# A planned four-batch attention-and-FFT-convolution kernel: complex products of the last batch summed on TensorE, a row scale moved into tables, split output tiles, and a new order of the work

## The chip, the cores and the metric

One core of a Trainium2 chip. The metric is the time of one execution of the program in device microseconds (us); lower is better. Times of a kernel are given as the median of its runs.

## The reference, cut to what matters

Four batches; 8 heads, 768 positions, head size 64. Attention is banded: each row sees the 8 first keys and the 96 keys up to itself, with a slope bias per head. Its output, 768 x 512 per batch, goes into a gated long convolution: a projection to three parts, a circular convolution of the second part with a filter along the sequence by a real FFT, a product of all three, and an output projection.

```python
scores = scale * np.matmul(q, k.transpose(0, 1, 3, 2)) + bias      # kept: global or local keys
a = softmax(scores); x = np.matmul(a, v)                           # -> (B, 768, 512)
proj = x @ w_proj; x1, x2, x3 = the three parts of proj
x2_conv = np.fft.irfft(np.fft.rfft(x2, axis=1) * np.fft.rfft(filter_fft, axis=0), axis=1)
out = (x1 * x2_conv * x3) @ w_out
```

## The kernel before, in words

The whole kernel is a graph of operations (class `Plan`) that is written out once and then issued in an order that stands in the source as a string, `ORDER` (L41). Each word names an operation by number and the engine that takes it: P is PE, A is ACT, V is DVE, G is POOL, S is SP. The digits behind a P are the PSUM banks that it takes. Every engine works through its own words strictly in this order; where an operand is not there, it waits and everything behind it on that engine waits too. A word such as `i5b2` is a filler (`busy`, L305): five matmuls of 512 columns on a buffer of zeros (`idle`, a part of the tile `uw`), whose result nobody reads. The order before has 12 such matmuls in four words, all in the first 16 us.

The stages of one batch, by names and lines:

- Loads (`load`, L324). Batch 0's first two pairs of heads of q and k come over SP's queue as float32 into a staging tile and are cast by DVE or ACT (`FIRST`, L206). All other loads go over POOL's queue, which casts to 16 bits as it moves; POOL's loads use eight semaphores in turn, so a load waits until the one eight places before it has landed. v of batch 0 comes in seven tiles, behind the pairs and the filter.
- Transposes of q and k on PE (`turned`, L677 and L680; the second form, 12 half-height matmuls a pair, is for pairs that POOL loaded), copied out to `QT` and `KT`. For the last batch SP's DMA transposes take their place.
- Scores on PE (L729), for batch 0 with the bias added by two further matmuls (`near`, L723), exponential on ACT (L744), mask product on DVE (L761; not for batch 0), in three groups of key tiles.
- Values (L779, L784) on PE, with a row sum; division on DVE or ACT (L803, L807), transposes back (L824) into `xT`.
- Gates (L902): four matmuls of 384 columns each, 64 groups in all; ACT scales one part out (`x1`), DVE multiplies it with the other, straight out of PSUM (L916, `g`).
- Butterflies on DVE (L831 on), the projection of the convolution branch (L965), copied out by L969 with a row scale `part` on four of six copies (tile `ab`), forward transform (L1081) against the tables `fold` and `fwd`, copied to `X` (L1084).
- Products with the filter's spectrum on DVE: p1 = X h1, p2 = X h2 (L1099, L1102), and the sums of the complex product X = p1 - p2, p1 + p2 (L1107, L1108).
- Inverse transform on PE (L989, L992): four matmuls of 128 columns a group, against the tables `inv` and `inr`; those come from PE transposes of the forward tables (`inverse_tables`, L523) and seven scaled copies. Then mixing on DVE, product with the gate (L1070), output projection (L1021): four matmuls of 512 columns a tile, six tiles a batch, copy (`ot`) and store over SP.

Setting up takes constant fills by memsets on DVE (`gaps`, `ones`, `second`, `part`) and sine tables on ACT.

Of the kernel before, what the change touches and what calls it, by code (L numbers as in the profile page):

```python
# [17 lines left out]
P = 128  # L18
NG = 8
# [9 lines left out]
def act(n):  # L29
    return 0.06 + n / 1200.0  # L30
# [11 lines left out]
0V 1V 2A 3G 4V 5V 30V 34V 45S 8V i3b5 17P0 18A 19V 57S 22P1 47S 12P2 49S 9V 32G 51S 55G 23A 58A 11V 13A 53G 7G  # L42
46V 20V 54G 33V 35G 50V 43V 24V 37V 21A i1b5 84P0 38A 48A 14V 60S 82P3 88P4 56G 85A 73G 61G 83A 52V 36V i3b5
96P3 116P67 15V 25V 98P01 89A 39V 97A 90P4 41V i5b2 94P5 16A 62G 26A 86P3 59V 44V 99A 10V 42V 91V 40A 117A 95V
92P2 63G 27V 122P45 156P01 31V 123A 93V 87V 104P67 65G 210V 120P45 29V 157A 102P23 105A 121A 67G 100P67 154P45
64G 103A 111P23 101A 66G 211V 245G 28V 212V 213V 155A 112V 244G 214V 113V 215V 118P01 152P67 119A 106P45 107V
150P01 129P23 216V 236G 246G 79A 153A 235G 151A 75A 243G 163P67 68G 130V 124P01 232G 108V 131V 109P4 77A 237G
158P23 114P5 110A 80A 164V 125V 165V 132P4 69G 166P6 126V 6V 217P7 115A 127P0 223P5 133A 219P4 159V 167V 346P6
238G 81A 160V 78A 220A 224A 348P1 128V 161P2 233G 138P0 218A 193V 194V 228P45 241G 134P7 140A 338P0 349V 231G
162A 136A 221P1 196V 347V 230A 240G 185V 381P67 222A 234G 359P23 340P5 339V 139P0 360A 135P1 195V 184V 419P23  # L50
187V 70G 382A 229A 141V 341V 361V 334P6 420A 172P0 76A 168P7 137V 174A 239G 472G 170A 353P23 421V 335V 375P45
242G 197V 471G 169P1 383V 74A 336P0 198V 146P6 186V 72G 376A 247G 462G 173P7 344P4 337V 354A 461G 342P0 249S
175V 250G 410P23 148A 345A 350P67 411A 142P5 188V 343V 199V 171V 189V 144V 351A 202P4 356P01 71G 412V 416P23
357A 254G 372P67 251G 253G 270P5 190V 252G 200V 373A 225P01 417A 201V 226A 191V 192V 257P6 227A 377V 258V 271A
463G 206V 470G 259P2 413P01 378P67 464G 260A 255G 272P5 207V 352V 283P2 465G 563P3 208A 374V 358V 414A 285P0
355V 204V 248S 379A 143P1 286A 284A 469G 564A 466G 273A 367P67 476G 415V 147P0 205A 209A 274P2 458G 380V 145V
203A 368V 263P3 149V 264A 362P01 276P5 261P4 275A 287V 277A 369V 363V 467G 418V 364V 468G 389P67 262A 278P2
573P3 384P45 265P0 390V 279A 370P2 288V 574A 180P1 266A 371A 391V 473G 475S 565P3 427P67 566A 280V 385V 281V
386V 282V 571P0 460G 567P2 256G 459G 697G 479G 422P45 182A 568A 268V 365P1 572A 423V 366A 428V 424V 176P3 267V
569P2 178A 570A 181P0 644P45 429V 177P1 291P2 645A 695G 183V 292A 430P6 387P7 179V 638P45 269V 431A 392P2 691G  # L60
425P3 388V 603P01 639A 301P6 297P7 393V 299P2 604A 457G 426V 300A 303P3 581P45 302A 582A 561P0 298A 704G 646V
293P2 640V 701G 688G 480G 449V 294A 687G 406P1 696G 394P6 703G 693G 584P45 448V 304A 289P7 396A 407P3 408V
295P6 451V 450V 698S 562A 705G 296A 398P2 585A 395P0 559P6 605V 477G 452V 409V 682G 586V 453V 400A 600P45
578P23 403P1 290A 560A 397V 305V 306V 481G 597P67 454V 601A 690G 598A 482P0 402P4 307V 579A 432P5 575P23 404A
483A 683G 474S 583V 405V 606P67 694G 308V 434A 495P4 576A 635P01 607A 641P23 399P5 456V 455V 444P6 636A 592P01
497P7 496A 577V 642A 446A 580V 498A 686G 508P4 637V 478G 700G 433P2 401V 593V 692G 309V 602V 587P67 699S 509A
510P3 702G 594A 435V 486P4 608V 588V 436P2 501P5 511A 438A 684S 310V 643V 311V 599V 589A 445P0 484P1 312V
499P2 485A 512V 500A 652P67 447V 689G 487A 653V 503P2 502A 488P3 609P01 313V 490P4 489A 504A 437P5 610V 685S
440P3 491A 654V 611A 505V 506V 614P67 615V 513V 439V 786S 616A 788S 319P2 442A 507V 647P01 441P5 612P4 785S
314V 648V 492V 613A 590P6 595P7 493V 649V 322P3 617P4 320A 655P2 596A 494V 315V 528P7 618A 591A 316P4 524P6  # L70
443V 784S 650P0 783S 529A 631P7 656A 323A 651A 790S 674V 317A 522P3 792S 520P2 673V 789S 523A 676V 787S 526P0
516P1 623P4 633A 517A 521A 625A 518P3 527A 624P7 514P2 675V 793S 796P45 632P1 515A 619P2 525A 626V 677V 797A
805P67 519A 621A 806A 634V 678V 719P4 802P23 799P01 530V 679V 531V 794S 620P5 622V 720A 669P4 734P6 627P5 681V
800A 827P01 803A 671A 735A 804V 821P23 828A 798V 680V 807V 629A 628P4 818P67 630V 822A 801V 824P01 532V 819A
708P5 813P23 820V 791S 795S 825A 814V 533V 706P4 815V 709A 707A 856P01 657P5 534V 712P4 857A 862P23 829V 823V
865P01 659A 859P67 670P5 863A 826V 535V 858V 860A 866A 710P2 672V 665P3 830P67 808P01 711A 861V 713A 714P2
864V 667A 831V 715A 723P4 809V 721P5 536V 832A 810V 732P2 724A 816P3 537V 817A 666P0 835P67 867V 717V 727P4
668V 722A 331P3 324S 728A 725P4 318S 658P5 811P0 538V 836V 733A 716V 660V 332A 873P23 726A 661P1 730V 837A
718V 874V 868P45 328P6 869V 321S 736V 325P7 663A 812A 662P0 729V 870V 838P1 875A 871P4 539V 833P5 333S 731V
876P2 839A 541P3 737V 834A 852P5 740P1 872A 877A 844P2 742P4 854A 752P5 326A 746P7 664V 741A 895V 894V 748P0  # L80
540V 896V 743A 753A 747A 749A 897V 898V 738P1 899V 547P4 750P7 744P5 745A 556P0 848P5 739A 751A 903P7 916P1
755V 900V 846A 327S 754V 901V 902V 845P2 904A 850A 917A 853P5 931P1 329A 756V 542A 929P6 932A 847V 920P7 757V
918P1 921A 930A 919A 907P7 924P6 330S 922P1 908A 550P2 905P7 543S 855V 923A 758V 911P1 933V 759V 925A 553P6
548A 906A 912A 934V 909P7 760V 927V 926V 557A 882P3 841P0 763V 928V 544P1 910A 884A 840P3 914V 956P7 941P4
545A 842A 551A 952P1 887P5 913V 761V 552S 915V 953A 554A 849P2 957A 762V 935P1 942A 851V 954P6 950P3 955A
939P7 951A 936A 764V 555S 959V 940A 546S 843V 765P4 937P3 777P2 774P0 886P1 958V 768P7 938A 549S 888A 944V
771P1 772A 943V 878P3 960V 945V 780P6 961V 946V 769A 558S 962V 947V 766A 963V 948V 778A 891P7 964V 889V 949V
880A 967V 965V 767S 968V 966V 883P1 775A 890P3 773S 781A 978V 770S 879P0 975P6 892A 980V 776S 893V 972P7 881V
885V 981V 969P1 976A 979V 782S 779S 973A 977S 982P0 983V 974S 970A 971S 984S 985P1 988P7 986A 991P6 987S 989V
992A 990S 993S  # L90
# [108 lines left out]
class Fused:  # L199
    PERIOD = 40.0  # L200
    NEAR = 3
    TWICE = frozenset()
# [3 lines left out]
    FIRST = (("k",0),("q",0),("k",1),("q",1))  # L206
# [29 lines left out]
    def buffers(self):  # L236
# [25 lines left out]
        self.inv = t("inv", [P, 4, P])  # L262
        self.uw = t("uw", [P, 4, 2, 2, P])
# [49 lines left out]
    def times(self, e, out, in_, c):  # L313
        if e == "A":
            self.nc.scalar.mul(out, in_, c)  # L315
        else:
            self.nc.vector.tensor_scalar(out, in_, c, None, op0=Alu.mult)

# [99 lines left out]
    def setup(self):  # L418
# [25 lines left out]
        def part(_):  # L444
            for i in range(2):
                c = math.sqrt(0.75) * (1.0 - 2.0 * i)
                v.memset(self.part[0:64, 2 * i:2 * i + 1], 1.0)
                v.memset(self.part[64:P, 2 * i:2 * i + 1], c)
                v.memset(self.part[0:64, 2 * i + 1:2 * i + 2], c)
                v.memset(self.part[64:P, 2 * i + 1:2 * i + 2], 1.0)  # L450
        g.op("V", 0.5, part, w=["part"], bias=-100)
# [4 lines left out]
        for i in range(4):  # L456
            et = self.E[i]

            def gaps(_, et=et):
# [4 lines left out]
            g.op("V", 0.42, gaps, w=[("E", i, c) for c in range(3)], name="gaps", bias=-3300)  # L464

    def tables(self):
# [3 lines left out]
        for a, n in enumerate((512, 256, 512)):  # L470
# [7 lines left out]
            g.op("V", dve(n, 2), lambda _, th=th: nc.vector.tensor_scalar(  # L478
                th, th, MAGIC, -float(S), op0=Alu.subtract, op1=Alu.mult), r=[("th", a)],
                w=[("th", a)], bias=-9898)  # L480
            g.op("V", dve(n), lambda _, th=th, b=b, n=n: nc.vector.tensor_add(
# [41 lines left out]
    def inverse_tables(self):  # L523
# [16 lines left out]
        for i, (dst, rows, lo, hi, k) in enumerate((  # L540
# [6 lines left out]
                 lambda e, dst=dst, rows=rows, lo=lo, hi=hi, k=k: self.times(  # L547
                     e, dst, corners(b.f16()) if lo is None else b.f16()[rows, lo:hi], k), use=[b],
                 w=[("inv", i)])

    def distances(self):


# [694 lines left out]
```

## Time and profile before

| what | value |
|---|---|
| median of 3 runs | 169.41 us (168.69 to 169.66) |
| the profiled execution's own time | 169.03 us |
| its span, first to last instruction | 167.3 us |
| outside the span | 1.73 us |
| mean granted TensorE clock | 0.996 |
| matmuls on PE, of these fillers | 1591, 12 |
| POOL's DMA issues | 84 |

A row of the chain of waits or of the timeline gives start, length, engine and line, and a count behind an x. The timeline's lengths are each instruction's own, and neighbours overlap in the pipeline; the chain's lengths are laid end to end, so it shows what one instruction adds to a dense stream. A row of the groups gives the count, the summed busy time, the mean of one in ns, and the idle time ahead of them.

### The profile page before, as it was taken

What the parts mean: (1) busy time and instruction counts of PE and PEld (TensorE: products, weight loads), DVE (VectorE), ACT (ScalarE), POOL (GpSimd) and SP (SyncE); (2) the same over time, 40 slices, a digit from 0 to 9 for tenths busy, and PEclk for the clock granted to TensorE, in tenths of its full rate; (3) what the DMA queues carried; (4) which work ended last, traced back from release to release, by engine and by line L of the source; (5) the groups of instructions that cost most, each with busy time, mean ns of one, the idle gap of its engine ahead of it and who ended that gap; (6) DMA issues with size and microseconds to landing.
All of it is one profiled execution on the core that took longest, in us unless ns stands there. A gap on an engine that the chain in (4) does not pass through costs nothing.

```text
span 167.3 us, 4244 instructions
## 1 busy us (share of the span) xinstructions
PE 158.4 (95%) x1591; PEld 93.5 (56%) x1591; DVE 154.2 (92%) x364; ACT 149.6 (89%) x324; POOL 76.3 (46%) x100
## 2 busy tenths in 40 slices
PE   7679999999999999999999999999999999999990
PEld 2335349666645777645556674455577644565550
DVE  4597999999999999999999999999989999999951
ACT  4949999999999999999999999999999879792851
POOL 7996699999769995989930000000000000000000
PEclk9999999999999999999999999999999999999998
DMA  4999999999999999999999645300010111052595
GB/s 157 246 183 200 153 151 165 162 171 174 166 159 125 120 119 155 155 155 144 149 143 153 77 95 136 149 0 0 4 65 4 65 60 66 4 217 97 205 358 191
DMA packets 84957, 22.14 MB, mean 132 GB/s; under 512 B 75585, under 2 KB 81993, under 8 KB 84937
## 3 DMA queue, kind: packets, MB, share of 16 engines
q0 software_dynamic: 72768, 11.92, 95.0%
q1 hardware_dynamic: 12168, 9.97, 20.0%
q8 instruction: 12, 0.20, 0.5%
q14 instruction: 9, 0.07, 0.1%
HBM read 25.40 MB, written 6.29 MB: 189 GB/s over the span
## 4 chain that ended last, share of the span: by engine, by line
PE 37%; POOL 20%; DMA 19%; ACT 12%; DVE 5%; issue 3%; POOLq 0%; ACTq 0%
DMA vn<-in_v_dram 13%; PE bank L902 11%; PE bank L1021 11%; POOL kn L327 7%; POOL qn L327 6%; DMA qn<-in_q_dram 5%; PE bank L965 5%; ACT xn L807 4%; POOL vn L327 3%; ACT E L744 3%; PE bank L989 2%; ACT ab L315 2%; ACT X L311 2%; POOL w L327 2%; PE bank L1081 2%
## 5 line engine op out<-in xcount | busy, mean ns | idle before, releaser
L902 PE MATMUL bank<-xT,w 128*128 128x384 f16 x256 | 49.5, 326 | 0.2 <-ACT ab L315 0.2
L744 ACT ACTIVATE E<-bank 128x864 f16<-128x864 f32 x48 | 42.1, 955 | 0.5 <-PE bank L729 0.3
L902 PEld LDWEIGHTS <-w 128*128 128x128 f16 x256 | 23.4, 98 | 16.3 <-issue 1.5
L327 POOL DMA_DIRECT2D vn<-in_v_dram x28 | 26.7, 965 | 3.5 <-DMA wo<-in_moe_w_out_dram 1.8
L1021 PE MATMUL bank<-wo,y 128*128 128x512 f16 (+1 forms) x100 | 23.4, 370 | 0.1
L327 POOL DMA_DIRECT2D kn<-in_k_dram x25 | 22.0, 900 | 3.0 <-PE bank L729 2.4
L327 POOL DMA_DIRECT2D qn<-in_q_dram x24 | 20.9, 883 | 1.3 <-DMA vn<-in_v_dram 1.2
L761 DVE TENSOR_TENSOR E<-E,mask 128x864 f16<-128x864 f16 x36 | 20.7, 601 | 0.0
L315 ACT ACTIVATE x<-bank 128x384 f16<-128x384 f32 x30 | 17.0, 572 | 2.0 <-PE bank L902 1.8
L315 ACT ACTIVATE ot<-bank 128x512 f32<-128x512 f32 (+1 forms) x23 | 13.4, 611 | 5.3 <-PE bank L1021 5.3
L916 DVE TENSOR_TENSOR g<-bank,x 128x384 f16<-128x384 f32 x32 | 17.4, 552 | 0.3 <-PE bank L902 0.2
L965 PE MATMUL bank<-w,xs 128*128 128x512 f16 x64 | 15.9, 379 | 0.1
L779 PE MATMUL bank<-vn,E 128*128 128x65 f16 x224 | 15.6, 193 | 0.3 <-ACT xn L807 0.2
L729 PE MATMUL bank<-QT,KT 64*128 64x216 f16 (+2 forms) x224 | 15.3, 243 | 0.1
L784 PE MATMUL bank<-vn,E 128*128 128x65 f16 x192 | 15.3, 193 | 0.0
L779 PEld LDWEIGHTS <-E 128*128 128x128 f16 x224 | 14.2, 97 | 2.0 <-issue 0.2
L311 ACT CAST eo<-bank 128x384 f16<-128x384 f32 x32 | 14.4, 551 | 0.5 <-PE bank L992 0.4
L311 ACT CAST X<-bank 128x512 f16<-128x512 f32 x24 | 14.5, 658 | 0.0
L1021 PEld LDWEIGHTS <-y 128*128 128x128 f16 x100 | 9.3, 98 | 8.8 <-issue 0.4
L784 PEld LDWEIGHTS <-E 128*128 128x128 f16 x192 | 13.3, 97 | 1.4 <-issue 0.7
L729 PEld LDWEIGHTS <-KT 64*128 64x128 f16 x224 | 7.8, 94 | 10.7 <-issue 8.2
L807 ACT ACTIVATE xn<-bank,rc 128x64 f16<-128x64 f32 x60 | 13.6, 480 | 0.0
(160 smaller groups left out, 334.1 us busy)
## 6 DMA issues: line engine op xcount, KB each, us to landing
out_dram<-ot SPq DMA_DIRECT2D x23, 256.0 KB
vn<-in_v_dram POOLq DMA_DIRECT2D x28, 120.0 KB, 7.3
kn<-in_k_dram POOLq DMA_DIRECT2D x16, 96.0 KB, 4.9
qn<-in_q_dram POOLq DMA_DIRECT2D x16, 96.0 KB, 4.9
w<-in_moe_w_proj_dram POOLq DMA_DIRECT2D x4, 256.0 KB, 5.3
kn<-in_k_dram POOLq DMA_DIRECT2D x7, 120.0 KB, 6.4
g<-in_moe_filter_fft_dram POOLq DMA_DIRECT2D x1, 768.0 KB, 9.3
qn<-in_q_dram POOLq DMA_DIRECT2D x6, 128.0 KB, 5.3
```

Source lines behind the costliest of these rows:

```text
L311: {"A": nc.scalar.copy, "V": nc.vector.tensor_copy, "G": nc.gpsimd.tensor_copy}[e](out, in_)
L315: self.nc.scalar.mul(out, in_, c)
L327: return self.g.op(eng, 0.57 + 0.00035 * nbytes[0] if eng == "G" else 0.5, lambda _: e.dma_start(dst, src), w=w, r=r, nbytes=nbytes, name= ...
L729: nc.tensor.matmul(bs[hh].f32()[:, off:off + w], self.KT[hs, hp, P * m:P * m + P], self.QT[hs, hp, KL * m:KL * m + w], start=(off == 0 and ...
L744: g.op("A", act(864), lambda _: nc.scalar.activation(eo, bs[0].two()[:, :, 0:432].rearrange("p h (m w) -> p h m w", m=2), Act.Exp, scale=s ...
L761: g.op("V", dve(864, 2), lambda _: nc.vector.tensor_mul(eo, eo, mk), r=[("mask", 2 * hp), ("mask", 2 * hp + 1)], w=[("E", hp, gi)], name=" ...
L779: nc.tensor.matmul(o[:, n, hh], ef[:, at:at + P], vt[:, t, 2 * hp + hh, 0:D + 1], start=first, stop=(t == 0), skip_group_check=True)
L784: nc.tensor.matmul(o[:, n, hh], ef[:, at:at + P], vt[:, t - 1, 2 * hp + hh, 0:D + 1], start=False, stop=True, skip_group_check=True)
L807: nc.scalar.mul(to[:, i, n], o[:, i, n, 0:D], rc[:, i, n])
L902: nc.tensor.matmul(bk.f32()[:, 0:h], self.w[:, c, o + P * j:o + P * j + P], self.xT[:, c, h * s:h * s + h], start=(c == 0), stop=(c == 3))
L965: nc.tensor.matmul(bk.f32(), src[:, c], w[:, c, DM:2 * DM], start=(c == 0), stop=(c == 3))
L1021: nc.tensor.matmul(bk.f32()[:, 0:n], y[:, c, P * t:P * t + P], self.wo[:, c, cs], start=(c == 0), stop=(c == 3))
```

## The change

Seven edits and a new order string:

1. `SUMPE = (3,)`: for batch 3 the sums of the complex product (L1107, L1108) are left out. Each inverse group takes p1 and p2 themselves: one matmul with p1 against `inv`, one with p2 against `inv` or a negated copy of it, `neg`, accumulated in PSUM. So 6 matmuls a group instead of 4, in 8 groups.
2. The row scale `part` leaves the copies `ab` and goes into the table `fold` (an operation `foldp`, four scalings of 128 x 128). It has to wait until the inverse tables were taken from the unscaled `fold`; the forward transforms wait for it.
3. `SPLIT = (3,4,5)`: the last batch's last three output tiles are issued as two PE operations of two matmuls a bank each, one for each half of y's channels.
4. `TWICE` for batch 3: ACT copies the second gate part out of PSUM, and DVE multiplies two 16-bit tiles in SBUF.
5. `FIRST` loses q of pair 1: it comes over POOL's queue in place of SP's, needs no cast, and takes the 12 half-height transposes.
6. Constant fills may run on ACT (`fill`), as may one step of the sine tables.
7. `ORDER` is new: on POOL the loads stand in another sequence; the inverse tables' transposes stand in the first PE operations; and the fillers are now 55 matmuls, in words of 1 and 2 at the start, and of 30, 8 and 14 later. PE has 1656 matmuls.

```diff
-0V 1V 2A 3G 4V 5V 30V 34V 45S 8V i3b5 17P0 18A 19V 57S 22P1 47S 12P2 49S 9V 32G 51S 55G 23A 58A 11V 13A 53G 7G
...
+0V 1V 2A 3G 45S 30A 47S 4V 34V 6A 9A 32G 56S 49S 5V i1b5 22P0 55G 23A 54G 7G 24A 10V 17P1 8V 33V 25V 51G 18A
+35G 19A 12P2 13A 46V 52G 37A 48V i2b5 83P0 38A 53G 81P3 72G 20V 26A 61G 63G 21A 14V 44V 50V 15V 39V 201P1 93P2
...
+353V i30b6 349P0 145P6 75A 174V 249S 412A 348V 141P2 346V 254G 357P45 350V 228A 417P01 147A 375V 253G 420P67
...
+359V 260P2 386V 365V 387V 462G 560P3 287A 479G 478G 285A 469G 261A i8b7 368P45 381V 279P0 366P1 472G 561A 473G
...
+i14b3 428P45 266P1 390P67 257G 265A 706G 567A 562P0 281V 267A 429V 388P3 391V 563A 179P2 430V 564P1 392V 176P4
...
-    TWICE = frozenset()
+    SPLIT = (3,4,5)
+    SUMPE = (3,)
+    TWICE = tuple((3,j,s) for j in range(4) for s in range(2))
...
-    FIRST = (("k",0),("q",0),("k",1),("q",1))
+    FIRST = (("k",0),("q",0),("k",1))
...
+    def fill(self, to, value):
+        n = to.shape[0]
+        zero = self.idle[0:n, 0:math.prod(to.shape[1:])]
...
+        self.nc.scalar.activation(to, zero, Act.Copy, bias=value, scale=1.0)
...
+        def scaled(e):
+            for s in range(4):
+                f = self.fold[:, (s + 2) % 4]
+                self.times(e, f, f, self.part[:, s:s + 1])
+        g.op("AV", {"A": 4 * act(P), "V": 4 * dve(P, 4)}, scaled, r=["part"], w=[("fwd", 3), "foldp"], name="foldp")
...
-                g.op("AV", self.evac(512), lambda e, i=i, t=t, k=k, bk=bk: self.times(
-                    e, self.ab[i][:, t, :], bk.f32(), k), use=[bk], r=["part"], w=[("ab", i, t)],
+                g.op("AV", self.evac(512), lambda e, i=i, t=t, bk=bk: self.copy(
+                    e, self.ab[i][:, t, :], bk.f32()), use=[bk], w=[("ab", i, t)],
...
-                            nc.tensor.matmul(to, X[:, s, cs],
+                            apart = b in self.SUMPE and not z
+                            k, c = s // 2, s % 2
+                            nc.tensor.matmul(to, self.p1[k][:, c, cs] if apart else X[:, s, cs],
                                              self.inr[:, s - 4] if z else self.inv[:, (s + 2) % 4],
                                              start=(n == 0), stop=True, skip_group_check=True)
+                            if apart:
+                                nc.tensor.matmul(to, self.p2[k][:, 1 - c, cs],
+                                                 self.inv[:, (s + 2) % 4] if c else self.neg[:, k],
+                                                 start=False, stop=True, skip_group_check=True)
...
+                parts = ((0, 1), (2, 3)) if last and t in self.SPLIT else (range(4),)
...
-                r=[("ab", i, t), ("fwd", 1 if s > 3 else 3)])
+                r=[("ab", i, t), ("fwd", 1) if s > 3 else "foldp"])
...
+        if b in self.SUMPE:
+            return
```

More of the change, by code (lines that the diff above doesn't have):

```diff
@@ L47 @@
[L47 to L51, printed above, removed]
@@ L442, in setup, with part @@
             None, op0=Alu.add), r=["irow"], w=["rows"], bias=-9988)
-        def part(_):
+        def part(e):
             for i in range(2):
                 c = math.sqrt(0.75) * (1.0 - 2.0 * i)
[L447 to L451, printed above, removed]
+                for rows, cols in ((slice(0, 64), (1.0, c)), (slice(64, P), (c, 1.0))):
+                    for x in range(2):
+                        to = self.part[rows, 2 * i + x:2 * i + x + 1]
+                        if e == "A":
+                            nc.scalar.activation(to, self.idle[rows, 0:1], Act.Copy, bias=cols[x], scale=1.0)
+                        else:
+                            v.memset(to, cols[x])
+        g.op("AV", {"A": 0.5, "V": 0.5}, part, r=["idle"], w=["part"], name="part", bias=-100)
         def ident(_):
@@ L457, in setup, with gaps @@
             et = self.E[i]
-            def gaps(_, et=et):
+            def gaps(e, et=et):
+                if e == "A":
+                    self.fill(et[:, :, 0:1488].rearrange("p h (m w) -> p h m w", m=6)[:, :, :, 216:248], 0.0)
+                    self.fill(et[:, :, 1456:1536], 1.0)
+                    return
                 et = et.bitcast(F32)
@@ L463, in gaps @@
                 v.memset(et[:, :, 728:768], ONES)
-            g.op("V", 0.42, gaps, w=[("E", i, c) for c in range(3)], name="gaps", bias=-3300)
+            g.op("AV", {"A": act(384) + act(160), "V": 0.38}, gaps, r=["idle"], w=[("E", i, c) for c in range(3)], name="gaps", bias=-3300)
     def tables(self):
@@ L477, in tables @@
                 w=[("th", a)], bias=-9899)
[L478 to L481, printed above, removed]
-                th, th, b.f32()[:, 0:n]), use=[b], r=[("th", a)], w=[("th", a)], bias=-9897)
+            g.op("AV", {"A": act(n), "V": dve(n, 2)}, lambda e, th=th: nc.vector.tensor_scalar(
+                th, th, MAGIC, None, op0=Alu.subtract) if e == "V" else nc.scalar.activation(
+                th, th, Act.Copy, bias=-MAGIC, scale=1.0), r=[("th", a)], w=[("th", a)], bias=-9898)
+            g.op("V", dve(n), lambda _, th=th, b=b, n=n: nc.vector.scalar_tensor_tensor(
+                th, th, -float(S), b.f32()[:, 0:n], op0=Alu.mult, op1=Alu.add), use=[b], r=[("th", a)],
+                w=[("th", a)], bias=-9897)
             o = (self.fold if a == 2 else self.fwd[:, 4 * a:4 * a + n // P]).rearrange("p s r -> p (s r)")
@@ L549, in inverse_tables @@
                  w=[("inv", i)])
+        def scaled(e):
[3 more added lines that the diff above has]
+        g.op("AV", {"A": 4 * act(P), "V": 4 * dve(P, 4)}, scaled, r=["part"], w=[("fwd", 3), "foldp"], name="foldp")
+        g.op("AV", {"A": 2 * act(P), "V": dve(2 * P, 4)}, lambda e: [self.times(
+            e, self.neg[:, n], self.inv[:, 2 - 2 * n], -1.0) for n in range(2)] if e == "A" else self.times(
+            e, self.neg[:, ::-1], self.inv[:, 0:4:2], -1.0), r=[("inv", i) for i in range(7)], w=["neg"], name="neg")
     def distances(self):
@@ L569, in distances, with second @@
         self.ahead = [g.op("G", 2.0, first, w=["dg"], bias=-9970)]
-        def second(_):
-            v.tensor_copy(dg[:, n:2 * n], dg[:, 0:n])
-            v.tensor_copy(dg[:, 2 * n:2 * n + 168], dg[:, 0:168])
-            v.memset(dg[0:NG, n:600], -HUGE)
-            v.memset(dg[0:NG, n:n + KL], -float(NL))
-            v.memset(dg[0:NG, 2 * n:2 * n + KL], -float(NL))
-            v.memset(dg[0:NG, 600:648], -float(NL))
-        g.op("V", dve(216, 4) + dve(168, 4) + 1.0, second, r=["dg"], w=["dg2"], bias=-3500)
+        def second(e):
+            put = self.fill if e == "A" else v.memset
+            self.copy(e, dg[:, n:2 * n], dg[:, 0:n])
+            self.copy(e, dg[:, 2 * n:2 * n + 168], dg[:, 0:168])
+            put(dg[0:NG, n:600], -HUGE)
+            put(dg[0:NG, n:n + KL], -float(NL))
+            put(dg[0:NG, 2 * n:2 * n + KL], -float(NL))
+            put(dg[0:NG, 600:648], -float(NL))
+        g.op("AV", {"A": 1.24, "V": 1.24}, second, r=["dg", "idle"], w=["dg2"], name="second", bias=-3500)
         g.op("V", 0.12, lambda _: v.memset(far, 0.0), w=["far"], bias=-3600)
@@ L956, in conv @@
         for i in range(2):
-            for t, (src, key, k) in enumerate((
-                    (self.xo[:, i], ("xo",), 1.0),
-                    (self.xs[:, 3 * i], ("xe", "xd"), self.part[:, 2 * i:2 * i + 1]),
-                    (self.xs[:, 2 - i], ("xe", "xd"), self.part[:, 2 * i + 1:2 * i + 2]))):
+            for t, (src, key) in enumerate((
+                    (self.xo[:, i], ("xo",)), (self.xs[:, 3 * i], ("xe", "xd")), (self.xs[:, 2 - i], ("xe", "xd")))):
                 bk = g.bank()
@@ L981, in conv @@
                     cs = slice(P * (2 * jp + jj), P * (2 * jp + jj) + P)
+                    apart = b in self.SUMPE
+                    src = [("p1", par), ("p2", par), ("X", 4 + par), "neg"] if apart else [
+                        ("X", s) for s in slots]
                     def turn(_, bk=bk, cs=cs, slots=slots, par=par):
@@ L1123, in load_first, with ones @@
         vt = self.vn[0]
-        def ones(_, vt):
+        def ones(e, vt):
+            if e == "A":
+                self.fill(vt[:, 0, :, self.D:], 1.0)
+                self.fill(vt[:, 1:, :, self.D:self.D + 2], 1.0)
+                return
             self.nc.vector.memset(vt[:, 0, :, self.D:].bitcast(F32), ONES)
@@ L1128, in load_first @@
         for i in range(2):
-            self.g.op("V", 0.4, lambda _, i=i: ones(_, self.vn[i]), w=[("vn1", i)], name="ones", bias=-4400 + 1400 * i)
+            self.g.op("AV", {"A": act(256) + act(96), "V": 0.33}, lambda e, i=i: ones(e, self.vn[i]), r=["idle"], w=[("vn1", i)], name="ones", bias=-4400 + 1400 * i)
         self.distances()
@@ L1180, in graph @@
         self.spectrum()
-        self.early = [x for x in g.ops if x.name in ("near", "angles", "mask")]
+        self.early = [x for x in g.ops if x.name in ("near", "angles", "mask", "gaps", "ones", "second", "part")]
         for b in range(self.B):
```

109 lines of the change are left out of this document (60 added, 49 removed).

## Prediction

> **What bounds the kernel now.** I read the page first: busy shares, the slices, the shares of the chain of waits.
>
> ```profile
> PE   7679999999999999999999999999999999999990
> ...
> DVE  4597999999999999999999999999989999999951
> ACT  4949999999999999999999999999999879792851
> ...
> PEclk9999999999999999999999999999999999999998
> ...
> PE 37%; POOL 20%; DMA 19%; ACT 12%; DVE 5%; issue 3%; POOLq 0%; ACTq 0%
> ```
>
> Three engines look full from slice 4 on, so shares decide nothing, and a busy PE is not PE at its peak. So the chain in order of time comes next. It runs through POOL's loads until 71.7 us, then from engine to engine, and from 110.8 us to the last matmul at 163.54 through PE alone. It also gives the price of one matmul in a dense stream.
>
> ```profile
> 72.32 0.48 PE bank L729 x8
> ...
> 111.81 0.80 PE bank L729 x18
> ...
> 115.39 0.06 PE bank L779 x2
> ...
> 126.13 1.14 PE bank L824 x20
> ...
> 150.02 1.73 PE bank L1021 x8
> ...
> 155.64 2.60 PE bank L902 x16
> 158.24 5.23 PE bank L1021 x28
> 163.54 0.38 ACT ot L315
> ```
>
> A matmul of 512 columns costs 1.73/8 = 0.216 us, of 384 columns 2.60/16 = 0.1625, of 128 columns 1.14/20 = 0.057, one for the values (65 columns) 0.06/2 = 0.03, a half-height score 0.80/18 = 0.044 to 0.48/8 = 0.060. The timeline of PE in the first 26 us shows the fillers and the start of the values:
>
> ```profile
> 9.82 1.49 PE L307 MATMUL bank<-uw 128*128 128x512 f16 x3
> ...
> 14.15 1.25 PE L307 MATMUL bank<-uw 128*128 128x512 f16 x5
> ...
> 25.27 0.20 PE L779 MATMUL bank<-vn,E 128*128 128x65 f16 x1
> ```
>
> At 25.27 the values of batch 0's third tile group begin.
>
> **The ruler.** I count PE's matmuls from that group on, in each program's own order, at these prices. Before: 256 of 384 columns (41.6 us), 224 of 512 (48.4), 8 of 256 (0.9, half price), 346 of 128 (19.7), 376 values (11.3), 168 half-height scores at 0.052, the middle (8.7; 7.4 to 10.1): 130.6 us. The trace takes 163.54 - 25.27 = 138.3. So PE loses about 7.7 us (6.3 to 9.0) to waits in that stretch, and since the chain is PE alone after 110.8, nearly all of it lies before that.
>
> **The change, part by part.**
>
> *Fillers and order.* 52 of the 55 new filler matmuls stand behind that group of values: 30 after 14 us of further work, then 8 and 14. They cost 52 x 0.216 = 11.2 us of PE, whatever else PE might be waiting for. They are free where PE would have waited; beyond that each pushes the end. 11.2 is more than the 7.7 that were lost before.
>
> Is there a wait of 6.5 us at the block of 30? The instruction behind it transposes k of pair 3 of batch 1. Its second load is POOL's 31st in the new order. The 31st before, issued at 32.97, took 4.8 us to land:
>
> ```profile
> 17.80 0.85 POOL L327 DMA_DIRECT2D kn<-in_k_dram  x1 [2.44 <-PE bank L729]
> ...
> 32.97 2.56 POOL L327 DMA_DIRECT2D kn<-in_k_dram  x3
> ...
> DMA to landing us min/median/max: 4.8/4.8/4.8
> ```
>
> That is 37.8 us. PE's work from the values group to the block is 14.1 us: 28 gate matmuls 4.55, 10 of 512 columns 2.16, 70 of 128 columns 4.0, 64 values 1.9, 28 scores 1.5. From 23.5 (below) PE reaches the block at 37.6, when the load is landing. So the block covers almost nothing of that load and holds back k's copy on DVE, the scores behind it, and everything that DVE has queued behind that copy. Later waits on DVE and ACT shrink by as much, since those two run ahead: that is how 11.2 us of fillers can swallow most of the 7.7.
>
> *The start.* Values of the third group need all seven tiles of v. The view of that tile in the first 30 us:
>
> ```profile
> L327 POOL DMA_DIRECT2D vn<-in_v_dram x7: 901/903/1197, 8.8 to 14.5; - x7
> ...
> DMA to landing us min/median/max: 8.8/9.1/9.9
> ```
>
> The last is issued at 14.5 and lands at 23.3. The new order puts the same pairs, filter and v tiles ahead of it; q of pair 1 only changes its queue. So 23.3 stays, and PE, which otherwise reaches the group earlier now (inverse tables and near scores stand ahead of it), starts at about 23.5 in place of 25.3: 1.8 us gained. POOL's extra issue is covered by the 2.44 us that POOL waited at 17.80; with that cover gone it costs 0.7 at each load behind.
>
> *Sums on PE, tables, gates.* The rows by form:
>
> ```profile
> L1108 DVE TENSOR_TENSOR X<-pp 128x512 f16<-128x512 f16 x8 | 3.4, 424 | 0.0
> L916 DVE TENSOR_TENSOR g<-bank,x 128x384 f16<-128x384 f32 x32 | 17.4, 552 | 0.3 <-PE bank L902 0.2
> L315 ACT ACTIVATE ab<-bank,part 128x512 f16<-128x512 f32 x16 | 11.5, 750 | 0.6 <-PE bank L965 0.6
> L315 ACT ACTIVATE ab<-bank 128x512 f16<-128x512 f32 x7 | 4.7, 671 | 0.7 <-PE bank L965 0.7
> L317 DVE TENSOR_SCALAR eo<-ident 128x128 bf16<-128x128 f16 x6 | 1.8, 320 | 0.0
> ```
>
> Batch 3's sums: four DVE instructions go, 4 x 0.42 = 1.7 us; 16 matmuls of 128 columns come, 0.9 us. The new gate product on 16-bit SBUF tiles of 384 columns lies under the 0.424 of the 512-column one above; I take 0.36, so 8 x (0.55 - 0.36) = 1.5 us of DVE, against eight more copies on ACT, whose last slices have room. Both savings fall into the stage that PE alone bounds, so DVE's 3.2 us bring nothing (from below zero to 3.2 if DVE still led), and the 0.9 counts in full. The row scale in the tables saves ACT 16 x 0.08 = 1.3 us and puts 4 x 0.32 = 1.3 us on DVE in the first 20 us, where it waits for loads; if not, 1.3. The forward transforms now wait for the scaled table; what is queued behind them on PE would wait too, but the table is due in the first 20 us, and a first transform needs batch 0's attention before it: 0. The inverse tables' 10 transposes move ahead of the values group: 10 x 0.057 = 0.6 us less in the counted stretch. ACT's fills lie in the first 5 us, beside the first loads. The split output tiles add no matmul; they let PE start on half of y, and at the end PE waits for nothing: 0, at most 0.3.
>
> **The sum.** Counted stretch after: 130.6 + 11.2 + 0.9 - 0.6 = 142.1 us. From 23.5, PE's last matmul ends at 165.6 plus the waits w that are left. w lies between 0 and the 7.7 of before. I take 2.0: little, because PE is now late against the others, yet not nothing, because DVE starves behind the block of 30 and hands on late. That gives 167.6, against 163.5. What follows the last matmul (167.3 - 163.5) and what lies outside the span (169.03 - 167.3) stay: 167.6 + 3.8 + 1.7 = 173.1; I forecast **173.0**. The median of the runs before, 169.41, lies 0.4 above the profiled execution, within their spread.
>
> **A rule that weighs on the start.** The fillers above show the clock: three at 9.82 take 1.49 us, 0.50 each; five at 14.15 take 1.25, 0.25 each. The granted clock reads 9 in both slices (the row PEclk), so this is not the throttle. The Trainium skill, "TensorE: Matmul & The Clock Gate", What's actually happening, says that PE runs at half its clock until about 3.4 us of sustained work, and falls back after as long an idle window; the trace agrees with the first half by these two rows, and no wait of PE here is long enough to show the second.
>
> **The rivals.**
>
> *Cold start.* Only 3 fillers stand in the first 20 us now, not 12. If PE is still at half speed while the near scores run, three of the near-score groups (two matmuls of 432 columns and four scores, 0.60 us at the prices above) take twice as long, and the values group starts 1.8 us late: 174.9. For: the two filler rows. Against: PE has slack until 23.3. The rule named above would have it so.
>
> *The waits stay.* If fillers and waits fall in different places, w is 5 to 7.7: 176.1 to 178.8. For: the block of 30 covers no load. Against: PE's operands are older now.
>
> *Faster.* v lands earlier. With 384 KB less on SP's queue, if its traffic was what made v's loads take 9 us in place of the 5 of later ones, the last v is there at 19.5, PE's dense stretch starts up to 3.8 us sooner, and with w at 0.5 the time is 19.7 + 142.1 + 0.5 + 5.5 = 167.8. It decides from a landing before 20 us. Against: the same bytes pass, on another queue.
>
> *No change.* The same, half as far: v at 21.5 and w at 0.5, 169.8. This is also the case in which the edits do no more than move work: fillers entirely in waits, DVE's savings unused.
>
> **How the numbers follow.** Forecast (w from 0.5 to 4, 171.6 to 175.1): 0.60. Cold start 0.12, waits stay 0.11, no change 0.09, faster 0.08. A measurement of this kernel can tell about 0.5% from no change, 168.56 to 170.26. Faster 0.08, same 0.09, slower 0.83. The range for 8 in 10 leaves out the faster case, part of no change and the end of the waits: 169.8 to 177.0.
>
> **What would show it.** In the trace after: PE's block of 30 fillers starts near 37.6 and takes 6.5 us, with the load behind it landed; DVE has an idle stretch there that it did not have; the values' third group starts at 23.3 to 24; from 45 us on PE's chain is dense, and its last matmul ends near 167.6. It is wrong if the block starts before 32 (then it fills a real wait), if v lands before 20, or if PE still idles several us after 60.

## The result, and the profile after

The changed kernel takes 175.73 us (median of 4 runs, 174.81 to 177.36); the kernel before, on the same chip, 169.05 us (4 runs, 168.20 to 169.66). The ratio is 1.041, with a 95% interval of 1.032 to 1.050: slower by 6.7 us. The profiled execution took 175.40 us, its span 173.6. A run more than 1.5% above the fastest of its kernel counts as slow; such runs are in the medians of this document, but not in the ratios.

Read the slices of the page first, with the shares of the chain under them (one digit is a 40th of the span, 4.3 us).

```profile
PE   6597998999999999999999999999999999999990
...
DVE  6699899994199693999999999999999999999960
ACT  8999998995099784999999999999999899987850
POOL 7996599999599902479998000000000000000000
...
PE 86%; ACT 8%; DVE 3%; issue 1%
```

PE has no hole. DVE and ACT have three that they did not have before: a deep one in slices 9 and 10, counted from 0 (39 to 48 us), and two smaller ones in slices 13 and 15. POOL nearly stops issuing loads around the last of them, in slices 14 to 16 (61 to 74 us). PE now has 86% of the chain of waits, in place of 37%. The chain in order of time (start, length, what) has the three late filler blocks in it, and the end of the kernel:

```profile
39.97 6.58 PE bank L310 x30
...
58.69 1.73 PE bank L310 x8
...
63.80 3.08 PE bank L310 x14
...
162.18 6.95 PE bank L1059 x36
169.16 0.42 DVE ot L320
```

The blocks take 6.58 + 1.73 + 3.08 = 11.4 us, and PE's last matmul ends at 162.18 + 6.95 = 169.13, against 163.5 before. What the others do beside the block of 30 stands in the timelines of DVE and of ACT; the number in brackets is the idle time before an instruction and what ended it.

```profile
40.22 0.74 DVE L314 COPY KT<-bank 128x720 f16<-128x720 f16 x3
46.99 0.75 DVE L314 COPY KT<-bank 128x720 f16<-128x720 f16 x3 [6.03 <-PE bank L707]
```

```profile
40.93 0.60 ACT L318 ACTIVATE h<-bank 128x512 f16<-128x512 f32 x1
47.57 0.49 ACT L318 ACTIVATE x<-bank 128x384 f16<-128x384 f32 x1 [6.04 <-PE bank L932]
```

The block begins at 39.97. DVE had work until 40.96 and ACT until 41.53, 1.0 and 1.6 us more; then both stood still for 6.0 us. The table of the stretch 40 to 48 us says the same. Its columns are the stretch, its length, and the busy time of PE, of its weight loads (PEld), of DVE, ACT and POOL, each with a count of instructions; behind them stand the granted clock, the share of the DMA engines and GB/s. First the kernel before, then the changed one.

```profile
40.00:48.00 8.00, 7.98 (x75) 4.45 (x72) 8.00 (x23) 8.00 (x14) 7.02 (x9) 1.00 2.07 168
```

```profile
40.00:48.00 8.00, 8.00 (x44) 3.87 (x43) 1.97 (x8) 1.97 (x4) 6.13 (x8) 1.00 1.84 174
```

Last, who made DVE wait between 25 and 110 us (total, times, longest), before and after:

```profile
DVE rc L808 <- PE bank L784: 0.7, 3, 0.3
DVE xab L840 <- ACT xT L311: 0.2, 1, 0.2
```

```profile
DVE KT L314 <- PE bank L707: 6.0, 1, 6.0
DVE rc L838 <- PE bank L814: 4.6, 3, 2.5
```

DVE's new waits add up to 10.6 us, nearly the length of the three blocks, and PE ends every one of them.

### The profile page after: what moved, and what is told of

It is laid out like the page before. It is cut to its first block, busy times and chain, and to the rows that moved or that the text cites. A ratio compares the mean times of both kernels' runs of the same rounds, so it can differ in the third digit from the quotient of the medians.

```text
span 173.6 us, 4360 instructions
## 1 busy us (share of the span) xinstructions
PE 164.0 (94%) x1656; PEld 99.2 (57%) x1656; DVE 152.3 (88%) x356; ACT 151.2 (87%) x327; POOL 76.9 (44%) x101
## 4 chain that ended last, share of the span: by engine, by line
PE 86%; ACT 8%; DVE 3%; issue 1%
PE bank L932 24%; PE bank L993 12%; PE bank L1059 12%; PE bank L310 7%; PE bank L759 6%; PE bank L854 4%; PE bank L809 4%; PE bank L707 3%; PE bank L1023 3%; PE bank L1124 3%; PE bank L814 3%; PE bank L753 2%; ACT E L774 2%; ACT KT L314 1%; PE bank L1030 1%; PE bank L690 1%
## 5 line engine op out<-in xcount | busy, mean ns | idle before, releaser
L932 PE MATMUL bank<-xT,w 128*128 128x384 f16 x256 | 48.2, 326 | 0.0
L774 ACT ACTIVATE E<-bank 128x864 f16<-128x864 f32 x48 | 41.0, 911 | 0.3
L932 PEld LDWEIGHTS <-w 128*128 128x128 f16 x256 | 23.9, 98 | 15.8 <-issue 0.3
L339 POOL DMA_DIRECT2D vn<-in_v_dram x28 | 26.0, 956 | 8.2 <-PE bank L1124 7.5
L1059 PE MATMUL bank<-wo,y 128*128 128x512 f16 (+1 forms) x100 | 22.6, 371 | 0.0
L339 POOL DMA_DIRECT2D qn<-in_q_dram x25 | 21.6, 875 | 1.6 <-PE bank L707 1.5
L809 PE MATMUL bank<-vn,E 128*128 128x65 f16 x224 | 15.0, 193 | 0.7 <-DVE xn L833 0.7
L314 ACT CAST ab<-bank 128x512 f16<-128x512 f32 x24 | 14.4, 632 | 0.8 <-PE bank L993 0.8
L814 PE MATMUL bank<-vn,E 128*128 128x65 f16 x192 | 14.8, 193 | 0.0
L310 PE MATMUL bank<-uw 128*128 128x512 f16 x55 | 13.4, 392 | 1.2 <-DVE warm L434 1.2
L833 DVE TENSOR_TENSOR xn<-bank,rc 128x512 f16<-128x512 f32 (+1 forms) x19 | 14.3, 772 | 0.1
L759 PE MATMUL bank<-QT,KT 64*128 64x216 f16 (+2 forms) x224 | 13.7, 242 | 0.0
```

What stands on the lines that cost most here:

```text
L310: self.nc.tensor.matmul(b.f32(), self.idle[:, 0:P], self.idle, start=True, stop=True)
L314: {"A": nc.scalar.copy, "V": nc.vector.tensor_copy, "G": nc.gpsimd.tensor_copy}[e](out, in_)
L339: return self.g.op(eng, 0.57 + 0.00035 * nbytes[0] if eng == "G" else 0.5, lambda _: e.dma_start(dst, src), w=w, r=r, nbytes=nbytes, name= ...
L759: nc.tensor.matmul(bs[hh].f32()[:, off:off + w], self.KT[hs, hp, P * m:P * m + P], self.QT[hs, hp, KL * m:KL * m + w], start=(off == 0 and ...
L774: g.op("A", act(864), lambda _: nc.scalar.activation(eo, bs[0].two()[:, :, 0:432].rearrange("p h (m w) -> p h m w", m=2), Act.Exp, scale=s ...
L809: nc.tensor.matmul(o[:, n, hh], ef[:, at:at + P], vt[:, t, 2 * hp + hh, 0:D + 1], start=first, stop=(t == 0), skip_group_check=True)
```

## The experiments

The theory that came out of the profile, F: the fillers stand where no operand is late; they push PE by their length, and DVE and ACT with it. Its rivals: the new order has these waits anyway and the fillers only stand in them (W); or only the block of 30 does harm, by starving DVE and POOL (D). A second question came with the first answer: which part of the change makes the rest faster? The median of the kernel before moved between 168.0 and 169.1 us from chip to chip, so kernels are compared by their ratios to it, and a difference of two ratios is given in us of 168.4.

| kernel | us, median | to before (95%) |
|---|---|---|
| the change | 175.73 | 1.041 (1.032 to 1.050) |
| no_late: no late fillers | 164.62 | 0.978 (0.973 to 0.983) |
| no_30: without the block of 30 | 170.20 | 1.010 (1.004 to 1.016) |
| only_30: without those of 8 and 14 | 171.87 | 1.019 (1.011 to 1.028) |
| before_30: before, and a block of 30 | 174.94 | 1.038 (1.031 to 1.045) |
| nl_sums: no_late, sums on DVE | 166.39 | 0.989 (0.984 to 0.993) |
| nl_gates: no_late, five gates as before | 167.68 | 0.997 (0.994 to 1.001) |
| nl_scale: no_late, row scale on ACT | 165.22 | 0.981 (0.976 to 0.986) |
| nl_split: no_late, whole output tiles | 164.70 | 0.978 (0.973 to 0.984) |
| nl_old4: no_late, these four undone | 169.51 | 1.008 (1.004 to 1.011) |
| a_sums: the change, sums on DVE | 177.88 | 1.057 (1.051 to 1.062) |
| nl_nofill: no_late, no filler at all | 164.64 | 0.977 (0.971 to 0.982) |
| nl_head: no_late, four early fillers more | 165.15 | 0.980 (0.978 to 0.983) |

### The late fillers

**no_late.** The three words go out of the written order, nothing else.

```diff
-353V i30b6 349P0 145P6
+353V 349P0 145P6
...
-261A i8b7 368P45
+261A 368P45
...
-566P2 i14b3 428P45
+566P2 428P45
```

> The changed kernel without the three late filler blocks (30, 8 and 14 matmuls of 512 columns, 52 x 0.216 = 11.2 us of PE); everything else of the change stays. Theory F (the fillers push PE and starve DVE, and cover no wait): nearly all of 11.2 us goes. PE's own sum would then end at about 155, so DVE sets the end: 152.3 us busy, 4.1 idle in the first 24 us and 5.7 idle after 140 add up to 162.1, with 1.8 outside the span 164; I expect 164 to 167, which is faster than the kernel before. Rival W (the new order waits there anyway and the fillers stand in those waits): 173 to 176, as the changed kernel. Rival D (only the block of 30 hurts): as F here.

Measured: 164.62 us, 11.1 less than the changed kernel (10.6 by the ratios) and faster than the kernel before. F and D hold, W falls. The slices of DVE and ACT have no hole any more, and the chain ends like this:

```profile
DVE  6599899999999999999999999999999999999960
ACT  8999999999998999999999999999998999997850
```

```profile
151.00 6.95 PE bank L1059 x36
157.97 0.42 DVE ot L320
```

PE's last matmul ends at 157.95, 11.18 us ahead of the changed kernel's 169.13: the fillers' 11.2 (52 x 0.216) to within 0.1. PE's own matmuls, from the values group that begins at 24.2 in both kernels, add up to 142.1 - 11.2 = 130.9 and would end at 155.1; it ends 2.8 later. With the fillers it is 24.24 + 142.1 = 166.3 and again 2.8 later. The profile itself names little of this as idle time of PE; between 24 and 110 us it lists, first for the changed kernel, then for no_late:

```profile
PE bank L809 <- DVE xn L833: 0.7, 1, 0.7
```

```profile
PE bank L809 <- DVE xn L833: 0.3, 1, 0.3
PE bank L809 <- DMA vn<-in_v_dram: 0.3, 1, 0.3
```

So the 2.8 is in the main short gaps and the error of the summed prices, and only the comparison counts: 11.2 us of fillers took away none of what PE loses. The expectation had DVE set the end; the chain of no_late runs through PE alone from 48 us on, with DVE as full beside it.

**no_30** and **only_30** take out one block, or the other two:

```diff
-353V i30b6 349P0 145P6
+353V 349P0 145P6
```

> The changed kernel without the block of 30 fillers alone; those of 8 and 14 stay. F: 30 x 0.216 = 6.5 us less, some of it given back because the blocks of 8 and 14 then meet other waits: 169 to 171. W: 174 or more. D (only this block starves DVE and POOL's queue): all of the loss goes, 164 to 167.

```diff
-261A i8b7 368P45
+261A 368P45
...
-566P2 i14b3 428P45
+566P2 428P45
```

> The changed kernel without the blocks of 8 and 14; that of 30 stays. F: 22 x 0.216 = 4.75 us less, or a little less than that: 171 to 172. W: 174 or more. D: no change, 175 to 176.

Measured: 170.20 and 171.87 us. By the ratios, taking out the 30 (6.5 us) gains 3.1% of 168.4, 5.2 us; taking out the 8 and 14 (4.75 us) gains 2.2%, 3.7 us. D falls, since the short blocks cost too. The intervals reach 1 to 1.6 us to either side. The traces are sharper: PE's last matmul ends at 162.2 in no_30 (155.25 + 6.96) and at 165.0 in only_30 (157.90 + 7.10), 6.9 and 4.1 us ahead of the changed kernel's. Together that is 11.0 of the 11.2, and each block costs its length to within 0.7.

**before_30.** The kernel before, with one such block at a similar place.

```diff
-173P7 344P4 337V
+173P7 i30b4 344P4 337V
```

> The kernel before with one block of 30 fillers (6.5 us of PE) put into PE's order ahead of a transposition of k of batch 1, at 41.3 us in its trace, where that operand has landed. F: PE's waits of 7.7 us in the whole of the rest can swallow some of the block, DVE starves behind it: 172 to 175.5, 3 to 6.5 us slower than the kernel before. W (fillers stand in waits): within 1 us of the kernel before.

Measured: 174.94 us, 3.8% (3.1 to 4.5) above the kernel before: 6.4 us of the block's 6.5. The kernel before had more than 7 us of waits on PE by the prediction's ruler, and the block took the place of hardly any.

### The other parts, with the late fillers gone

Without the fillers the change gains 2.2%. These kernels put one part at a time back, in the same order but for the words named, and then four of them.

**nl_sums.** The sums of batch 3 are formed by DVE again, right behind p2, and the inverse reads X. For this, two words of DVE change places with a neighbour (922V with 923V, 934V with 935V), and the same in a_sums and nl_old4.

```diff
-src = [("p1", par), ("p2", par), ("X", 4 + par), "neg"] if apart else [
-    ("X", s) for s in slots]
+src = [("X", s) for s in slots]
...
-apart = b in self.SUMPE and not z
+apart = False
...
+def second(_):
+    nc.vector.tensor_mul(p2, xs, self.h2[:, n:n + 1].to_broadcast([P, 2, DM]))
+    if b in self.SUMPE:
+        sums(_)
```

> The changed kernel without its late fillers (164.6 us), with batch 3's sums put back on DVE: 16 matmuls of 128 columns go from PE (0.9 us), four sums of 0.42 us come back to DVE (1.7 us). Theory P (PE alone bounds the last part): 0.9 us faster, 163.7. Rival V (DVE leads; its savings are what made the waits of the new order small): 1 to 1.7 us slower, 165.6 to 166.3.

Measured: 166.39 us, 1.8 slower, with intervals that do not touch. Rival V holds: the sums on PE are a gain, not a loss. The stretch from 140 to 150 us shows how (columns as above): first no_late, then nl_sums, and the waits of PE and its weight loads after 115 us in nl_sums.

```profile
140.00:150.00 10.00, 10.00 (x90) 6.57 (x89) 9.99 (x25) 8.43 (x20) 0.00 (x0) 1.00 0.01 2
```

```profile
140.00:150.00 10.00, 8.73 (x68) 5.04 (x67) 9.93 (x24) 7.31 (x17) 0.00 (x0) 1.00 0.01 2
```

```profile
PEld L1020 <- DVE X L1150: 1.1, 2, 0.9
PE bank L1020 <- DVE X L1150: 0.7, 1, 0.7
...
PEld L1020 <- DVE X L1151: 0.5, 2, 0.2
```

In no_late PE and DVE both show no idle time there, 10.00 and 9.99 of 10. With the sums back on DVE, DVE stays at 9.93 and PE is busy for 1.3 us less, waiting for just those sums (X, lines 1150 and 1151).

**nl_gates.** Five of the eight new gate products of batch 3 are formed straight from the bank; four of their words for DVE move up behind the words of the left-out copies. For the other three this could not be done in this order, since their banks are taken again before DVE has x1.

```diff
-lambda _: nc.scalar.copy(x3, pts[1].f32()[:, 0:h]), use=[pts[1]],
+lambda _: None if (j, s) in self.ALONE else nc.scalar.copy(x3, pts[1].f32()[:, 0:h]), use=[pts[1]],
...
-g.op("V", dve(h, 2), lambda _: nc.vector.tensor_mul(x3, x3, x1), r=[key], w=[ko], name="g")
+g.op("V", dve(h, 2), lambda _: nc.vector.tensor_mul(x3, pts[1].f32()[:, 0:h] if alone else x3, x1),
+     use=[pts[1]] if alone else [], r=[key], w=[ko], name="g")
```

> The same kernel (164.6 us) with five of the eight new gate products of batch 3 done as before: DVE multiplies straight from the bank (0.55 in place of 0.31 to 0.36 us, about 1.1 us of DVE more), and ACT's five copies of 0.48 us go. Theory P: no change, 164.3 to 164.9. Rival V: about 1 us slower, 165.6.

Measured: 167.68 us, 3.1 slower; V expected 1. The waits of PE after 115 us name what the sizes of the instructions leave out:

```profile
PE bank L1024 <- DVE g L944: 1.8, 1, 1.8
...
PE bank L1060 <- DVE g L944: 0.8, 1, 0.8
```

The first wait is for a bank: the inverse `751P0` wants bank 0, in which the matmuls of the gate `842P0` lie until DVE has multiplied. With ACT's copy the bank was free long before. The group rows of no_late give the sizes (busy, mean ns of one): a product straight from the bank, and one on ACT's copy.

```profile
L946 DVE TENSOR_TENSOR g<-bank,x 128x384 f16<-128x384 f32 x24 | 12.8, 552 | 0.4 <-PE bank L932 0.2
...
L944 DVE TENSOR_TENSOR g<-g,x 128x384 f16<-128x384 f16 x8 | 2.6, 351 | 0.0
```

So a copy brings DVE 0.2 us, 1.0 us for the five, and a bank that comes free early; the wait of 1.8 us for that one bank is more than the five savings.

**nl_scale** puts the row scale back.

```diff
-self.times(e, f, f, self.part[:, s:s + 1])
+pass
...
-e, self.ab[i][:, t, :], bk.f32()), use=[bk],
+e, self.ab[i][:, t, :], bk.f32(), self.part[:, 2 * i + t - 1:2 * i + t] if t else 1.0), use=[bk], r=["part"],
```

> The same kernel (164.6 us) with the row scale back in ACT's copies of ab (16 x 0.08 = 1.3 us of ACT more, spread over four batches) and the scaling of the tables left out (four short DVE instructions in the first 20 us less). Theory P: no change, 164.3 to 164.9. A rival (ACT is as full as PE from 25 to 110 us, so its 1.3 us counts): 1 to 1.3 us slower, up to 165.9.

Measured: 165.22 us, 0.6 slower, between the two expectations; the intervals overlap, so this part stays open between 0 and about 1 us.

**nl_split** brings the whole output tiles back.

```diff
-project(_, cc),
+project(_, {(0, 1): (), (2, 3): range(4)}.get(cc, cc)),
```

> The changed kernel without its late fillers (164.6 us), with the last three output tiles in one piece again: their eight matmuls of each pair of halves stand together where the second half stood. The prediction's step (PE waits for nothing at the end; 0, at most 0.3): 164.3 to 164.9. A rival (near the end DVE leads and hands y over by halves, so a whole tile waits for its second half while PE has no other work): 0.5 to 1.5 us slower, 165.1 to 166.1.

Measured: 164.70 us, no difference.

**nl_old4** is the four edits above together.

> The same kernel (164.6 us) with four parts of the change undone together: sums on DVE, five gate products straight from the bank, row scale on ACT, output tiles in one piece. What is left of the change is the new order with 3 fillers and the moved fills. Theory P (the new order took the waits from 7.7 to 2.8 us): 163.5 to 165. Rival V (the four parts together took them): back to 167.5 to 168.5, as the kernel before.

Measured: 169.51 us, 4.9 slower than no_late and 0.8% slower than the kernel before; V's 167.5 to 168.5 was still too low. So what is then left of the change, the new order above all, with three of the eight gate copies, the moved fills and q of pair 1, is no gain; the sums, the gates and perhaps the scale carry it. The fills and q of pair 1 were not undone by themselves. Whether these would gain as much in the old order was not tried; their operations have other numbers there, and the order would have to be written anew.

**a_sums** tests the same in the kernel as it was changed, fillers and all, with the edit of nl_sums.

> The changed kernel with all its fillers (175.7 us), with batch 3's sums back on DVE (16 matmuls less on PE, 0.9 us; four DVE sums more, 1.7 us). The prediction's step (PE alone bounds that stage, so the 0.9 counts in full and DVE's saving brings nothing): 174.8. The rival that the run without the fillers bore out (DVE leads the last stage): 1.8 us slower, as there, 177.5; the fillers stand 80 us earlier and should not matter to it.

Measured: 177.88 us, 2.2 slower than the changed kernel. The prediction's step fails here as it did without the fillers, and with the other sign.

### The fillers at the start

**nl_nofill** drops the last three fillers; **nl_head** has six in place of two at 4.3 us, so seven in all.

```diff
-56S 49S 5V i1b5 22P0
+56S 49S 5V 22P0
...
-37A 48V i2b5 83P0
+37A 48V 83P0
```

> The same kernel (164.6 us) without the last three fillers too, those in the first 5 us. If PE's clock has to be raised by work ahead of the first transpositions at 7.2 us, these run longer at half speed (18 of them by 0.05 us, and the tables' six: 1 us at most later for the first scores): up to 165.6. If the head is paced by ACT's exponentials (12.96 to 24.9 us, 0.79 each), no change: 164.3 to 164.9.

```diff
-37A 48V i2b5 83P0
+37A 48V i6b5 83P0
```

> The changed kernel without its late fillers (164.6 us), with four fillers more (six in place of two) at 4.3 us, where PE waits 1.86 us for DVE's first copy of k. At half speed four take 4 x 0.42 = 1.7 us and at full speed 0.9. If fillers are free where PE really waits: 164.3 to 164.9, the first transposition still at 7.2; if PE's clock then is up earlier, the first 12 transpositions take 0.5 per six in place of 0.76, which would bring 0.5 us at most, and only if PE sets the head. If fillers cost their length wherever they stand: 165.5 to 166.3.

Measured: 164.64 us, no difference; and 165.15 us, between the two expectations, with an interval that overlaps no_late's. The times alone do not decide the second, but the trace does. PE in nl_head, from 4 us on:

```profile
4.27 2.74 PE L310 MATMUL bank<-uw 128*128 128x512 f16 x6
7.18 0.82 PE L707 MATMUL bank<-ident,kn 128*128 128x128 f16 x6 [0.17 <-DVE kn L314]
...
9.81 0.55 PE L710 MATMUL bank<-ident,qn 128*64 128x128 f16 x12
...
11.18 0.54 PE L753 MATMUL bank<-eo 128*128 128x432 bf16 x2
```

The six fillers fit into the wait, and the transposition starts at 7.18 as in the changed kernel. These six, at least, held nothing up at their place.

## Why the prediction was right, and where it was wrong

The direction was right, and so was the cause that the prediction gave for the loss, more fillers than waits; the forecast of 173.0 us was 2.4 short of the profiled 175.4. The loss itself, 6.7 us, is nearly twice the 3.6 that 173.0 makes against 169.41. Term by term, against the sum 23.5 + 142.1 + 2.0 + 3.8 + 1.7 = 173.1: 24.24 + 142.1 + 2.8 + 4.5 + 1.8 = 175.4.

**The block of 30: right.** It started at 39.97, not 37.6, and took 6.58 us: 0.7 of the delay came from the start, 0.7 from PE's wait at 26.59 shown below, and the rest because PE's work ahead of it took longer than priced. The load behind it was there: the view of the tile kn around POOL's 31st load shows the last of two issues at 33.0 and 4.5 us to landing, 37.6.

```profile
L339 POOL DMA_DIRECT2D kn<-in_k_dram x2: 897/902/906, 32.2 to 33.0; - x2
...
DMA to landing us min/median/max: 4.5/4.6/4.7
```

DVE's idle stretch came as forecast; that ACT would stand still as long was not forecast.

**"Later waits on DVE and ACT shrink by as much": wrong.** This was to let 11.2 us of fillers swallow most of 7.7. They swallowed nothing: w, what PE loses by the same ruler, is 2.8 us with the late fillers and 2.8 without. It came out near the value taken (2.0) for another reason than the one given: the other parts of the change had made it small already. That is luck. With w at 2.0 the fillers were to cost 11.2 - 5.7 = 5.5 us and the rest of the change was to gain 1.5 (1.8 + 0.6 - 0.9); on PE's last matmul the fillers cost 11.2 and the rest gained 5.5 (163.5 to 157.95). The two errors, 5.7 and 4.0, cancel for the most part. The picture behind the step was that DVE and ACT would run ahead while PE is busy with fillers. They could not, because they had 1.0 and 1.6 us of work that did not hang on PE. So the delay of one was handed to all three.

The 7.7 itself is 0.6 too high. The group of values that needs all of v has 24 matmuls, and before it begins at 25.84; at 25.27 begins the group of 16 ahead of it, which the count of 376 leaves out.

```profile
25.84 0.19 PE L779 MATMUL bank<-vn,E 128*128 128x65 f16 x1
```

That makes 163.54 - 25.84 - 130.6 = 7.1 us, and the start gained 1.6 (25.84 to 24.24).

**"Both savings fall into the stage that PE alone bounds, so DVE's 3.2 us bring nothing, and the 0.9 counts in full": wrong.** The sums on PE were worth 1.8 us (2.2 with the fillers), where the step had them cost 0.9; five of the eight gates were worth some 3. The evidence for the step was that the chain went through PE alone after 110.8 us. But a chain names the engine that did not wait; it does not say that the others had slack. The row of the kernel before that would have told, from 140 to 150 us:

```profile
140.00:150.00 10.00, 10.00 (x77) 5.99 (x75) 10.00 (x20) 9.01 (x20) 0.00 (x0) 1.00 0.19 72
```

PE 10.00 and DVE 10.00 of 10: neither engine shows any idle time. An edit that moves work between them is priced against both.

**The start: 0.7 short.** The last load of v was issued at 15.0, not 14.5, and landed 8.9 us later, at 23.9, not 23.3; the values group began at 24.24, directly behind the values ahead of it.

```profile
L339 POOL DMA_DIRECT2D vn<-in_v_dram x7: 903/909/930, 9.6 to 15.0; - x7
...
DMA to landing us min/median/max: 8.9/9.1/9.6
```

```profile
24.24 0.19 PE L809 MATMUL bank<-vn,E 128*128 128x65 f16 x1
...
26.59 0.19 PE L809 MATMUL bank<-vn,E 128*128 128x65 f16 x1 [0.72 <-DVE xn L833]
```

POOL's extra issue, priced at 0 behind a cover and 0.7 without it, is the obvious reason for the later issue, but no run took it away. The cover could not serve here: POOL waited at 17.80, behind the loads of v, and the extra issue stands ahead of them. Nor did PE wait for v in this execution: v was there 0.3 us earlier, and PE's own stream, almost without a gap since the first exponential freed a bank at 15.2, set the start. Where v came later, PE did wait for it: in nl_nofill the last load, issued at 14.9, landed at 25.1, and PE's waits list 0.2 us for v. The second row is the largest wait that is left on PE: 0.72 us for DVE, in the values right behind.

**The tail: 0.7 short.** From the last matmul to the end of the span it is 173.6 - 169.13 = 4.5 us, against 3.8 before. no_late has 162.5 - 157.95 = 4.55 as well, but no_30 has 167.7 - 162.2 = 5.5 and only_30 170.3 - 165.0 = 5.3, with the same end of the program. So this term moves by 1 us from one execution to another, and the 0.7 is not shown to come from the change.

**Split 0 and scale 0:** the first was right, the second is not refuted.

**The rivals.** Cold start fell: the values group began 24.24 - 23.5 = 0.7 late, not 1.8, and the first pair of near scores already took 0.54 us in the changed kernel, where the pair at 15.20 takes 0.53.

```profile
11.38 0.54 PE L753 MATMUL bank<-eo 128*128 128x432 bf16 x2
```

"The waits stay" came near in its time (176.1) but not in its mechanism, since w is 2.8 us and not 5 to 7.7. "Faster" and "no change" needed v to land before 22 us; it landed at 23.9.

## What to carry to other kernels

In these kernels filler work was free only inside a wait that the trace shows at that place; elsewhere it cost about its full length, and since the engines feed each other with little more than a microsecond in hand, all of them paid it. A chain through one engine does not give the others slack: read the busy time of every engine in that stretch before pricing an edit that moves work from one to another at nothing. And when a copy empties a bank earlier, look for who wants that bank: that was worth more here than the instruction it made shorter.

## What was not expected of the hardware

What PE's early work cost in these runs depended on how long PE had been at work, and none of it reached the end. PE without any filler, in nl_nofill, at the moment at which nl_head has the row at 9.81 above:

```profile
9.79 0.85 PE L708 MATMUL bank<-ident,qn 128*64 128x128 f16 x12
...
12.10 0.90 PE L751 MATMUL bank<-eo 128*128 128x432 bf16 x2
```

Twelve transpositions take 0.85 us here and 0.55 in nl_head, and the first scores' pair of matmuls at 12.10 still takes 0.90, where it takes 0.54 at 11.18 in nl_head. So the seven fillers brought PE to full speed more than 2 us sooner. The row PEclk of the two pages reads 9 in all slices and does not show it. The Trainium skill, "TensorE: Matmul & The Clock Gate", What's actually happening, says that the array goes to full clock after a busy window of about 3.4 us, and that the windows run freely. The runs agree in kind: in nl_head PE was at full speed at 9.81, 5.5 us after the six fillers began at 4.27, which lies between one such window and two. Counted from 1.97, when it began on matmuls of a single row, it is 7.8 us, more than two; the runs do not tell which work counts.

But the exponentials on ACT begin at the same time in both, first nl_nofill, then nl_head:

```profile
14.23 0.89 ACT L772 ACTIVATE E<-bank 128x864 f16<-128x864 f32 x1
```

```profile
14.26 0.89 ACT L774 ACTIVATE E<-bank 128x864 f16<-128x864 f32 x1
```

So a faster PE at the start was worth nothing in this kernel: the first exponential, on ACT, does not come sooner for it.
